# Attention and two MLPs on one Trainium2 core: the shared sums of a seven-product gate and value stage, kept in PSUM by copies on ACT instead of added on DVE

## The chip, the cores and the metric

The kernel runs on one core of one Trainium2 chip. The metric is the device time of one execution in microseconds (us); lower is better. All times below are in us unless marked ns. The engines are TensorE (PE; its weight loads are shown as PEld), VectorE (DVE), ScalarE (ACT), GpSimd (POOL) and SyncE (SP), whose queue issues the DMAs.

## The reference

With N = 6016 tokens and C = 256 channels, attention over the channels is followed by a squared-ReLU MLP (256 to 2048 to 256) and by a gated MLP (256 to 1536 to 256) with an RMS norm ahead of it:

```python
qn = q / (np.linalg.norm(q, axis=1, keepdims=True) + 1e-06)
kn = k / (np.linalg.norm(k, axis=1, keepdims=True) + 1e-06)
a = softmax(kn.transpose(0, 2, 1) @ qn / tau)      # 256 x 256
x = (v @ a).reshape(6016, 256)
h = np.maximum(x @ w_in, 0.0)
x = h * h @ w_out
xn = x / np.sqrt(np.mean(x * x, axis=-1, keepdims=True) + 1e-06) * rms_g
g = xn @ w_gate
out = (g / (1 + np.exp(-g)) * (xn @ w_val)) @ w_out2
```

Every product is carried at nearly full float32 precision by three TensorE matmuls: each operand is split in a high and a low part, and high times high, high times low and low times high are summed in PSUM.

## The kernel before

The tokens are cut into 12 blocks: ten of 512 tokens and two of 448 (lines 46 to 52). The attention runs first, then the first MLP block by block (`mlp1`), then the second MLP (`mlp2`) over six pairs of blocks. The order of all work is written out by hand (line 54); every engine runs its instructions in the order in which the code issues them.

**The second MLP.** A pair p holds two blocks of equal size n, the two columns of a 2 x 2 block product: gate and value (the rows) of two token blocks, over two halves of the channels. Seven products stand for the eight of the plain form: A11, S2, S3, S1, A12, A22 and S4 (line 882). Their operands on the token side are prepared by `pair_steps` (lines 841 to 877), written to DRAM as a high and a low part, and read back by `fetch` (lines 895 to 906). `group(f)` (line 926) runs the seven products of one of the 12 slices of 128 hidden features. A product is three matmuls into one PSUM bank (`product`, line 930; line 933).

The four results are the two gate columns and the two value columns. Two of them need a sum that is shared: u = A11 + S2, and u + S3. In the kernel before, ACT copies A11 out of its bank (p1, line 955), DVE adds S2 (u, line 961), adds u and S3 and S1 to form the second value (h22, lines 963 and 967), adds u and S3 + A22 to form the first value (h21, line 973), multiplies it by the first SiLU (line 974), and adds u and S1 + S4 to form the second gate (h12, line 978). A12 accumulates onto A11, A22 onto S3 and S4 onto S1, by matmuls that do not start anew (lines 969, 972, 976).

**What comes after a group.** A group's second half is done by steps that stand in the next group (`late`, line 948): ph1 and pl1 split h21 in a high part (ACT, line 984) and a low part (DVE, line 988), silu2 applies SiLU to h12 (ACT, line 994), p2 multiplies it onto h22 (DVE, line 997) and splits its high part (ACT), pl2 its low part (DVE). Only then can the down projection use them: a "down" is three matmuls (lines 103 to 105) for one of two token blocks and one of two output halves, so a group makes four. They are put on a list and taken off it in the four `down_slot` calls of each group (line 886); one that is made in group f is taken in the later slots of group f+1 or in the first slots of group f+2. When the last group of a pair is taken down, ACT copies each of the four results out of PSUM (line 922), which falls in the first two groups of the next pair.

**The start of the second MLP (pair 0).** Three downs of the first MLP are still pending; the first three slots of group 0 take them, six matmuls of 448 columns each (line 764). The fourth slot of group 0 and the first two of group 1 are empty. The token operands of the seven products have the numbers 0 (for A11), 1 (S2), 2 (S3), 3 (S1), 4 (A12), 5 (A22) and 6 (S4), the first argument of `product`. They are loaded through SP's queue, each by two DMAs (high and low part): 0, 1 and 2 are issued in the last block of the first MLP (line 1136), 3 to 6 behind them at its end (line 1146). SP works in order. The load of index 2 writes tiles o4 and o5, which the norm of the block before last holds until its last scaling on DVE (line 833). After each of the first eight groups of pair 0, two more steps are done (lines 1150 to 1169): the norm of the last block (`norm_steps`, lines 776 to 839: copies and squares on ACT after group 0, sum, transposition and reduction on DVE after group 1, the mean by a small matmul, the square root on ACT and its spreading after group 2, the scaling on DVE after group 3), then the preparation of the last pair's operands after groups 4 to 7 (`pair_steps`). Each of those seven preparations is a cast on ACT (line 856), a subtraction on DVE (line 863) and a write to DRAM (line 866); the tile has two buffers, so ACT can cast the third only when the first has been written.

**PSUM.** Eight banks: four rotate under the name mm (line 63), two each hold the two sums of the down projection.

Of the kernel before, what the change touches and what calls it, by code (L numbers as in the profile page):

```python
# [14 lines left out]
ALU = mybir.AluOpType  # L15
# [4 lines left out]
NB = 512  # L20
# [5 lines left out]
def attn_moe_kernel(ctx: ExitStack, tc, q, k, v, tau, w_in, w_out, w_gate, w_val, w2, rms_g, out):  # L26
# [8 lines left out]
    nc = tc.nc  # L35
# [27 lines left out]
    def mm():  # L63
        return ps.tile([P, NB], F32, tag="mm", name="mm", bufs=4)
# [24 lines left out]

    few = wp.tile([P, P], F32, name="few")  # L90
    eps, g_sb, tau_sb, rden = few[:, 0:1], few[:, 16 : 16 + KC], few[:, 32:33], few[:, 48 : 48 + KC]
    nc.gpsimd.memset(eps, 1e-6)


    wo_h = wp.tile([P, NF1, C], F32R, tag="wo_h", name="wo_h")
# [675 lines left out]

    SLOT = ((0, 4), (2, 6))
    xst, x_dram = {}, {}
    norm_small = ctx.enter_context(tc.tile_pool(name="ns", bufs=1, reuse_waits="tile"))

    def norm_steps(b, y):
# [3 lines left out]
        st = {}  # L780
# [32 lines left out]
            )  # L813

        def s4():
            ms = mm()[:, :G]
            nc.tensor.matmul(ms, mw, st["sm"][0], start=True, stop=True)

            def root():
                x, r = st["sm"]  # L820
                nc.scalar.activation(out=x, in_=ms, func=AF.Sqrt, bias=eps)
                nc.vector.reciprocal(out=r, in_=x)

            return root
# [55 lines left out]


    A11, A12, A22, S1, S2, S3, S4 = range(NC7)
    slots = {"n": 0}
    waiting = []

    def down_slot():
# [18 lines left out]
        for j in range(2):  # L905
            nc.sync.dma_start(out=f32(ops[i][j]), in_=x_dram[p][:, i, j, :n])

    def mlp2(p, ops, after_product, after_group):
        n = blocks[2 * p][1]
        o = {}  # L910
        left = []
# [14 lines left out]
        def group(f):  # L926
            c = gv[f // 2]
            fs = slice(f % 2 * P, (f % 2 + 1) * P)

            def product(i, a, bank, start):  # L930
                xh, xl = ops[i]
                for j, (hl, x) in enumerate(((0, xh), (1, xh), (0, xl))):
                    nc.tensor.matmul(bank, c[:, hl, a, fs], x, start=start and j == 0, stop=j == 2,  # L933
                                     skip_group_check=not start)
                after_product(f, i)


            b0, b1 = mm()[:, :n], mm()[:, :n]
            if f % 2:
                b0, b1 = b1, b0  # L940
            b2, b3 = mm()[:, :n], mm()[:, :n]
            pu = wp.tile([P, 2, NB], F32, tag="raw", name="pu", bufs=NRAW)[:, :, :n]
            p1, u = pu[:, 0], pu[:, 1]
            hp = wp.tile([P, 2, NB], F32, tag="gp", name="hp", bufs=2)[:, :, :n]
            h21, h22 = hp[:, 0], hp[:, 1]
            old = left.pop() if left else {}

            def late(k):
                if k in old:
                    old[k]()  # L950

            add, dve = nc.vector.tensor_tensor, nc.vector.tensor_tensor
            product(0, A11, b0, True)
            late("ph1")
            nc.scalar.copy(out=p1, in_=b0)
            late("silu2")
            late("pl1")
            down_slot()
            product(1, S2, b1, True)
            late("p2")  # L960
            add(out=u, in0=b1, in1=p1, op=ALU.add)
            product(2, S3, b2, True)
            add(out=h22, in0=b2, in1=u, op=ALU.add)  # L963
            late("pl2")
            down_slot()
            product(3, S1, b3, True)
            add(out=h22, in0=b3, in1=h22, op=ALU.add)
            down_slot()
            product(4, A12, b0, False)
            sg1 = wp.tile([P, NB], F32, tag="dg", name="sg", bufs=3)[:, :n]  # L970
            nc.scalar.activation(out=sg1, in_=b0, func=AF.Silu)  # L971
            product(5, A22, b2, False)
            add(out=h21, in0=b2, in1=u, op=ALU.add)  # L973
            dve(out=h21, in0=sg1, in1=h21, op=ALU.mult)  # L974
            down_slot()
            product(6, S4, b3, False)
            h12 = wp.tile([P, NB], F32, tag="dg", name="sg", bufs=3)[:, :n]
            add(out=h12, in0=b3, in1=u, op=ALU.add)
            new = {}
            parts = {}  # L980

            def hi(t, x):
                parts[t] = work("sh", n), work("sl", n)
                nc.scalar.copy(out=parts[t][0], in_=x)  # L984

            def lo(t, x):
                ph, pl = parts[t]
                dve(out=pl, in0=x, in1=f32(ph), op=ALU.subtract)  # L988
                due = slots["n"] + 2
                waiting.extend((due, down(f, t, d, ph, pl)) for d in range(KC))  # L990

            new["ph1"] = lambda: hi(0, h21)
            new["pl1"] = lambda: lo(0, h21)
            new["silu2"] = lambda: nc.scalar.activation(out=h12, in_=h12, func=AF.Silu)

            def p2():
                dve(out=h22, in0=h12, in1=h22, op=ALU.mult)
                hi(1, h22)

            new["p2"] = p2  # L1000
            new["pl2"] = lambda: lo(1, h22)
            left.append(new)
            after_group(f)
# [150 lines left out]
    for p in range(NP):  # L1154
# [16 lines left out]
                for i in range(3):  # L1171
                    fetch(p + 1, i, nxt)

        group, left, rest, finish = mlp2(p, ops, after_product, after_group)
        if tails:
            left.append(tails[0])
        for f in range(NF2):
# [42 lines left out]
```

## Time and profile before

| what | value |
|---|---|
| median of 3 runs | 1152.65 us (1152.17 to 1152.69) |
| the profiled execution | 1152.68 us |
| its span in the profile | 1150.9 us |
| TensorE, DVE, ACT busy | 98%, 75%, 58% of the span |
| granted TensorE clock, mean | 0.996 |
| first MLP ends, second MLP begins | about 595.6 us |

The profile shows one execution. Its span runs from the first to the last instruction; the execution's own time is 1.8 us longer. In the rows of its views, an instruction or a group of equal neighbours stands with its start, its duration, engine, line, operation and the tiles that it writes and reads; in square brackets stands how long the engine was idle before it and what ended that. Matmuls overlap: a matmul's duration is longer than the distance to the next one. Tiles of the program: mm is a PSUM bank of the products, acc one of the down sums, sh and sl the high and low part of a hidden tile, hp holds h21 and h22, pu holds p1 and u, sg a SiLU or h12, o and xs are loaded operands, gv the weights of gate and value, xp a prepared operand and xd its copy in DRAM.

### The profile page before, as it was taken

How to read it: one execution, taken by the hardware profiler on the slowest of the kernel's cores; microseconds unless marked ns; L12 is line 12 of the kernel's file. 1: busy time of each engine (PE TensorE's matmuls, PEld its weight loads, DVE VectorE, ACT ScalarE, POOL GpSimd, SP SyncE). 2: the span in 40 equal slices, each digit the busy share in tenths (PEclk: the TensorE clock that was granted, in tenths of full speed). 3: DMA queues.
4: the chain of work that ended last, by engine and by line, in shares of the span. 5: the costliest groups of instructions: out<-in, count | busy, mean ns of one | idle time of the engine just before them, and what ended most of it. 6: DMA issues, size and time to landing. Idle time of an engine off the chain costs nothing.

```text
span 1150.9 us, 14618 instructions
## 1 busy us (share of the span) xinstructions
PE 1123.1 (98%) x5220; PEld 942.2 (82%) x5220; DVE 868.9 (75%) x1372; ACT 666.4 (58%) x1166; POOL 57.5 (5%) x91
## 2 busy tenths in 40 slices
PE   8999989999999999999999899999999999999996
PEld 7978868878888888889977678888888888888995
DVE  6987868877787665565658787887877887877875
ACT  7687878678687676676665344334334334334432
POOL 1021130201201000000000000000000000000000
PEclk9999999999999999999999999999999999999999
DMA  9852332442351320120146222302302302202101
GB/s 290 229 144 87 89 87 74 131 152 83 110 174 46 109 75 17 56 90 1 76 160 277 81 87 73 92 1 74 92 1 74 92 1 74 72 14 64 25 13 32
DMA packets 99289, 101.23 MB, mean 88 GB/s; under 512 B 57616, under 2 KB 74256, under 8 KB 98704
## 3 DMA queue, kind: packets, MB, share of 16 engines
q1 hardware_dynamic: 99216, 100.29, 27.5%
q8 instruction: 41, 0.67, 0.2%
q14 instruction: 32, 0.26, 0.1%
HBM read 65.21 MB, written 35.06 MB: 87 GB/s over the span
## 4 chain that ended last, share of the span: by engine, by line
PE 82%; DVE 7%; ACT 5%; DMA 3%; SPq 2%; issue 2%; POOL 1%; DVEq 0%; ACTq 0%; POOLq 0%
PE mm L933 27%; PE acc L104 11%; PE acc L103 11%; PE acc L105 11%; PE mm L104 6%; PE mm L103 6%; PE mm L105 6%; DMA xd<-xp 1%; SPq L379 1%; ACT o L739 1%; DMA qraw<-in_k_dram 1%; DVE dg L141 1%; DVE sl L751 1%; ACT o L743 1%; PE mm L541 1%
## 5 line engine op out<-in xcount | busy, mean ns | idle before, releaser
L933 PE MATMUL mm<-o,gv 128*128 128x512 f32 (+1 forms) x1188 | 309.8, 388 | 4.7 <-DVE hp L963 3.2
L933 PEld LDWEIGHTS mm<-o,gv 128*128 128x128 f32 x1188 | 222.1, 188 | 51.7 <-DVE hp L963 5.5
L751 DVE TENSOR_TENSOR sl<-o,sh 128x512 fp32r<-128x512 f32 (+1 forms) x192 | 133.5, 695 | 112.7 <-ACT sh L744 99.5
L984 ACT CAST sh<-hp 128x512 fp32r<-128x512 f32 (+1 forms) x144 | 88.2, 612 | 151.4 <-DVE hp L974 97.4
L104 PE MATMUL acc<-sl,wo_h 128*128 128x512 f32 (+1 forms) x384 | 149.0, 388 | 3.6 <-DVE sl L751 3.6
L103 PE MATMUL acc<-sh,wo_h 128*128 128x512 f32 (+1 forms) x384 | 149.6, 389 | 1.6 <-ACT sh L747 1.5
L105 PE MATMUL mm<-o,m_l 128*128 128x512 f32 (+1 forms) x384 | 148.1, 386 | 0.3 <-DVE m_l L678 0.3
L105 PE MATMUL acc<-sh,wo_l 128*128 128x512 f32 (+1 forms) x384 | 148.2, 386 | 0.2
L103 PE MATMUL mm<-o,m_h 128*128 128x512 f32 (+1 forms) x384 | 148.0, 385 | 0.0
L104 PE MATMUL mm<-o,m_h 128*128 128x512 f32 (+1 forms) x384 | 148.0, 385 | 0.0
L739 ACT ACTIVATE o<-mm 128x512 f32<-128x512 f32 (+1 forms) x192 | 112.4, 585 | 60.0 <-PE mm L105 55.6
L971 ACT ACTIVATE sg<-mm 128x512 f32<-128x512 f32 (+1 forms) x72 | 42.5, 590 | 140.9 <-PE mm L933 140.8
L103 PE MATMUL acc<-sh,w_h 128*128 128x512 f32 (+1 forms) x288 | 111.3, 386 | 2.4 <-ACT sh L984 2.4
L104 PE MATMUL acc<-sl,w_h 128*128 128x512 f32 (+1 forms) x288 | 111.4, 387 | 0.7 <-DVE sl L988 0.6
L105 PE MATMUL acc<-sh,w_l 128*128 128x512 f32 (+1 forms) x288 | 110.9, 385 | 0.0
L988 DVE TENSOR_TENSOR sl<-hp,sh 128x512 fp32r<-128x512 f32 (+1 forms) x144 | 96.4, 669 | 10.4 <-ACT sh L984 6.3
L973 DVE TENSOR_TENSOR hp<-mm,pu 128x512 f32<-128x512 f32 (+1 forms) x72 | 48.9, 679 | 64.4 <-PE mm L933 64.4
L104 PEld LDWEIGHTS acc<-sl,wo_h 128*128 128x128 f32 x384 | 72.1, 188 | 19.3 <-DVE sl L751 6.7
L103 PEld LDWEIGHTS acc<-sh,wo_h 128*128 128x128 f32 x384 | 72.1, 188 | 16.4 <-ACT sh L747 2.8
L105 PEld LDWEIGHTS mm<-o,m_l 128*128 128x128 f32 x384 | 72.1, 188 | 14.6 <-DVE m_l L678 1.1
L105 PEld LDWEIGHTS acc<-sh,wo_l 128*128 128x128 f32 x384 | 72.1, 188 | 14.2 <-DVE wo_l L170 0.9
L103 PEld LDWEIGHTS mm<-o,m_h 128*128 128x128 f32 x384 | 72.1, 188 | 13.6
(139 smaller groups left out, 1770.6 us busy)
## 6 DMA issues: line engine op xcount, KB each, us to landing
xd<-xp SPq DMA_DIRECT2D x35, 512.0 KB, 2.6
o<-xd SPq DMA_DIRECT2D x58, 256.0 KB, 4.4
raw<-in_moe_w_out_dram SPq DMA_DIRECT2D x14, 512.0 KB, 3.7
gv<-gvd SPq DMA_DIRECT2D x4, 1792.0 KB, 14.7
gvd<-gp SPq DMA_DIRECT2D x12, 512.0 KB, 3.4
out_dram<-ot SPq DMA_DIRECT2D x40, 128.0 KB, 2.5
qraw<-in_q_dram SPq DMA_DIRECT2D x13, 384.0 KB, 4.8
qraw<-in_k_dram SPq DMA_DIRECT2D x13, 384.0 KB, 5.9
```

The costliest lines, as they stand in the source:

```text
L103: nc.tensor.matmul(o, wh, xh, start=start, stop=False)
L104: nc.tensor.matmul(o, wh, xl, start=False, stop=False)
L105: nc.tensor.matmul(o, wl, xh, start=False, stop=stop)
L141: nc.vector.tensor_tensor(out=gi, in0=gi, in1=self.raw[:, 0::2], op=ALU.add)
L379: nc.sync.dma_start(out=rows[:, g, kk], in_=src[:, kk])
L739: nc.scalar.activation(out=r, in_=o, func=AF.Relu)
L751: nc.vector.tensor_tensor(out=sl, in0=s, in1=f32(sh), op=ALU.subtract)
L933: nc.tensor.matmul(bank, c[:, hl, a, fs], x, start=start and j == 0, stop=j == 2, skip_group_check=not start)
L971: nc.scalar.activation(out=sg1, in_=b0, func=AF.Silu)
L973: add(out=h21, in0=b2, in1=u, op=ALU.add)
L984: nc.scalar.copy(out=parts[t][0], in_=x)
L988: dve(out=pl, in0=x, in1=f32(ph), op=ALU.subtract)
```

## The change

The products of a group are issued in another order, and the shared sums stay in PSUM.

- New order: A11, S1, slot, S2, A12, slot, S3, slot, slot, A22, S4. Before: A11, slot, S2, S3, slot, S1, slot, A12, A22, slot, S4.
- The four banks: b0 holds A11, then A11 + A12. The other three take turns (over `slots["g"] % 3`) as bh (S1, then S1 + S4), bu (u) and bv (u + S3, then u + S3 + A22).
- ACT copies b0 into bu, and S2's matmuls accumulate onto it without starting anew; ACT then copies bu into bv, onto which S3 and later A22 accumulate, and copies u out to SBUF. After S3 it copies bv out (w). DVE then adds S1 and w (h22), multiplies bv with the first SiLU (h21) and adds S1 + S4 and u (h12): three operations in place of six.
- In the first group of pair 0 alone, one matmul each opens bu and bv before anything accumulates there.
- The mean of the last block's norm, a matmul of 14 columns after group 2, no longer takes a bank of its own out of the rotation: ACT writes zeros to 16 columns of b0 of group 2 after that group's first SiLU, and the small matmul accumulates there. The zeros come from one more memset on POOL at the start.

```diff
--- before.py
+++ after.py
@@ -89,7 +89,9 @@
 
     few = wp.tile([P, P], F32, name="few")
     eps, g_sb, tau_sb, rden = few[:, 0:1], few[:, 16 : 16 + KC], few[:, 32:33], few[:, 48 : 48 + KC]
+    zeros = few[:, 64 : 64 + NB // 32]
     nc.gpsimd.memset(eps, 1e-6)
+    nc.gpsimd.memset(zeros, 0.0)
 
 
     wo_h = wp.tile([P, NF1, C], F32R, tag="wo_h", name="wo_h")
@@ -771,6 +773,8 @@
 
     SLOT = ((0, 4), (2, 6))
     xst, x_dram = {}, {}
+
+    spare = {2: None}
     norm_small = ctx.enter_context(tc.tile_pool(name="ns", bufs=1, reuse_waits="tile"))
 
     def norm_steps(b, y):
@@ -813,8 +817,12 @@
             )
 
         def s4():
-            ms = mm()[:, :G]
-            nc.tensor.matmul(ms, mw, st["sm"][0], start=True, stop=True)
+            if b < NBLK - 1:
+                ms = mm()[:, :G]
+                nc.tensor.matmul(ms, mw, st["sm"][0], start=True, stop=True)
+            else:
+                ms = next(iter(spare.values()))[:, :G]
+                nc.tensor.matmul(ms, mw, st["sm"][0], start=False, stop=True, skip_group_check=True)
 
             def root():
                 x, r = st["sm"]
@@ -880,7 +888,7 @@
 
 
     A11, A12, A22, S1, S2, S3, S4 = range(NC7)
-    slots = {"n": 0}
+    slots = {"n": 0, "g": 0}
     waiting = []
 
     def down_slot():
@@ -905,7 +913,7 @@
         for j in range(2):
             nc.sync.dma_start(out=f32(ops[i][j]), in_=x_dram[p][:, i, j, :n])
 
-    def mlp2(p, ops, after_product, after_group):
+    def mlp2(p, ops, after_product, after_group, spare):
         n = blocks[2 * p][1]
         o = {}
         left = []
@@ -935,12 +943,14 @@
                 after_product(f, i)
 
 
-            b0, b1 = mm()[:, :n], mm()[:, :n]
-            if f % 2:
-                b0, b1 = b1, b0
-            b2, b3 = mm()[:, :n], mm()[:, :n]
+
+
+            turn3 = slots["g"] % 3
+            slots["g"] += 1
+            b0, *b = [mm()[:, :n] for _ in range(4)]
+            bh, bu, bv = b[turn3:] + b[:turn3]
             pu = wp.tile([P, 2, NB], F32, tag="raw", name="pu", bufs=NRAW)[:, :, :n]
-            p1, u = pu[:, 0], pu[:, 1]
+            u, w = pu[:, 0], pu[:, 1]
             hp = wp.tile([P, 2, NB], F32, tag="gp", name="hp", bufs=2)[:, :, :n]
             h21, h22 = hp[:, 0], hp[:, 1]
             old = left.pop() if left else {}
@@ -949,33 +959,43 @@
                 if k in old:
                     old[k]()
 
-            add, dve = nc.vector.tensor_tensor, nc.vector.tensor_tensor
+            add, dve, cp = nc.vector.tensor_tensor, nc.vector.tensor_tensor, nc.scalar.copy
             product(0, A11, b0, True)
+            if p > 0 or f > 0:
+                cp(out=bu, in_=b0)
             late("ph1")
-            nc.scalar.copy(out=p1, in_=b0)
             late("silu2")
             late("pl1")
+            product(3, S1, bh, True)
             down_slot()
-            product(1, S2, b1, True)
+            if p == 0 and f == 0:
+
+                for x in (bu, bv):
+                    nc.tensor.matmul(x, c[:, 0, A11, fs], ops[0][0], start=True, stop=True)
+                cp(out=bu, in_=b0)
+            product(1, S2, bu, False)
+            cp(out=bv, in_=bu)
+            cp(out=u, in_=bu)
             late("p2")
-            add(out=u, in0=b1, in1=p1, op=ALU.add)
-            product(2, S3, b2, True)
-            add(out=h22, in0=b2, in1=u, op=ALU.add)
-            late("pl2")
-            down_slot()
-            product(3, S1, b3, True)
-            add(out=h22, in0=b3, in1=h22, op=ALU.add)
-            down_slot()
             product(4, A12, b0, False)
             sg1 = wp.tile([P, NB], F32, tag="dg", name="sg", bufs=3)[:, :n]
             nc.scalar.activation(out=sg1, in_=b0, func=AF.Silu)
-            product(5, A22, b2, False)
-            add(out=h21, in0=b2, in1=u, op=ALU.add)
-            dve(out=h21, in0=sg1, in1=h21, op=ALU.mult)
+            if f in spare:
+
+                spare[f] = b0[:, : NB // 32]
+                cp(out=spare[f], in_=zeros)
+            late("pl2")
             down_slot()
-            product(6, S4, b3, False)
+            product(2, S3, bv, False)
+            cp(out=w, in_=bv)
+            add(out=h22, in0=bh, in1=w, op=ALU.add)
+            down_slot()
+            down_slot()
+            product(5, A22, bv, False)
+            dve(out=h21, in0=bv, in1=sg1, op=ALU.mult)
+            product(6, S4, bh, False)
             h12 = wp.tile([P, NB], F32, tag="dg", name="sg", bufs=3)[:, :n]
-            add(out=h12, in0=b3, in1=u, op=ALU.add)
+            add(out=h12, in0=bh, in1=u, op=ALU.add)
             new = {}
             parts = {}
 
@@ -1171,7 +1191,7 @@
                 for i in range(3):
                     fetch(p + 1, i, nxt)
 
-        group, left, rest, finish = mlp2(p, ops, after_product, after_group)
+        group, left, rest, finish = mlp2(p, ops, after_product, after_group, spare if p == 0 else ())
         if tails:
             left.append(tails[0])
         for f in range(NF2):
```

## Rows read from the trace of the kernel before

**Rows 1.** The page: TensorE's busy time, and its granted clock in 40 slices.
```profile
PE 1123.1 (98%) x5220; PEld 942.2 (82%) x5220; DVE 868.9 (75%) x1372; ACT 666.4 (58%) x1166; POOL 57.5 (5%) x91
...
PEclk9999999999999999999999999999999999999999
```

**Rows 2.** Busy time by stretch: stretch, length, engines' busy us (instructions), clock, DMA.
```profile
595.60:607.20 11.60, 10.05 (x41) 6.85 (x40) 4.74 (x8) 4.82 (x9) 0.00 (x0) 1.00 0.82 287
607.20:667.20 60.00, 54.01 (x229) 41.78 (x228) 48.48 (x80) 26.47 (x47) 0.00 (x0) 1.00 0.36 150
667.20:1138.00 470.80, 470.80 (x2119) 397.58 (x2118) 378.21 (x601) 191.83 (x342) 0.00 (x0) 1.00 0.18 52
```

**Rows 3.** Timeline of a steady group: start, duration, engine, line, operation, count.
```profile
906.91 0.62 ACT L984 CAST sh<-hp 128x512 fp32r<-128x512 f32 x1 [1.54 <-DVE hp L974]
...
907.43 0.58 ACT L955 COPY pu<-mm 128x512 f32<-128x512 f32 x1
...
911.30 1.52 PE L933 MATMUL mm<-o,gv 128*128 128x512 f32 x6
912.24 0.60 ACT L971 ACTIVATE sg<-mm 128x512 f32<-128x512 f32 x1 [2.32 <-PE mm L933]
...
912.66 0.39 PE L103 MATMUL acc<-sh,w_h 128*128 128x512 f32 x1
```

**Rows 4.** Timeline, first group of pair 0.
```profile
595.60 0.86 PE L933 MATMUL mm<-o,gv 128*128 128x512 f32 x3
...
596.29 0.36 PE L103 MATMUL acc<-sh,wo_h 128*128 128x448 f32 x1
...
596.66 4.88 SPq L906 DMA_DIRECT2D o<-xd  x10
...
597.50 0.86 PE L933 MATMUL mm<-o,gv 128*128 128x512 f32 x3
...
599.52 1.05 PE L933 MATMUL mm<-o,gv 128*128 128x512 f32 x3 [1.15 <-DMA o<-xd]
```

**Rows 5.** Timeline, fourth group of pair 0: a product that waits for DVE.
```profile
627.32 0.69 DVE L963 TENSOR_TENSOR hp<-mm,pu 128x512 f32<-128x512 f32 x1
...
628.07 0.98 PE L933 MATMUL mm<-o,gv 128*128 128x512 f32 x3 [0.98 <-DVE hp L963]
...
628.88 0.40 PE L103 MATMUL acc<-sh,w_h 128*128 128x512 f32 x1
```

**Rows 6.** Groups of instructions by line, 667.2 to 1138.0: busy us, mean ns.
```profile
L967 DVE TENSOR_TENSOR hp<-mm,hp 128x512 f32<-128x512 f32 (+1 forms) x64 | 43.0, 671 | 0.0
...
L955 ACT COPY pu<-mm 128x512 f32<-128x512 f32 (+1 forms) x64 | 36.6, 572 | 0.0
...
L922 ACT COPY ys<-acc 128x512 f32<-128x512 f32 x20 | 11.7, 586 | 12.4 <-PE acc L105 12.4
```

**Rows 7.** Tile xd, 597.9 to 598.1: the two loads of S1's operand.
```profile
L906 SPq DMA_DIRECT2D o<-xd x2: 382/404/426, 597.6 to 598.0; - x2
...
DMA to landing us min/median/max: 4.0/4.3/4.5
```

**Rows 8.** Timeline, fourth and seventh group of pair 0: a table load, a blocked ACT.
```profile
623.96 1.28 ACT L994 ACT_TABLE_LOAD   x1
...
650.01 0.56 ACT L856 CAST xp<-xst 128x448 fp32r<-128x448 f32 x1 [5.50 <-DMA xd<-xp]
...
651.15 0.50 PE L103 MATMUL acc<-sh,w_h 128*128 128x512 f32 x1 [1.20 <-ACT sh L984]
```

**Rows 9.** The page's DMA issues: KB each, median us to landing.
```profile
xd<-xp SPq DMA_DIRECT2D x35, 512.0 KB, 2.6
```

**Rows 10.** Timeline of TensorE near the start of the span.
```profile
8.28 0.50 PE L541 MATMUL mm<-hl 128*128 128x256 f32 x2 [1.91 <-DVE hl L517]
```

**Rows 11.** Busy time by stretch near the start, columns as in rows 2.
```profile
5.30:8.60 3.30, 1.39 (x10) 1.18 (x11) 1.22 (x1) 2.19 (x3) 1.04 (x5) 1.00 0.92 306
8.70:12.00 3.30, 3.30 (x18) 3.30 (x17) 1.83 (x2) 1.57 (x3) 0.00 (x0) 0.50 1.07 362
```

## The prediction

> **What bounds the kernel now.** I read the page's busy times first: TensorE is busy for 98% of the span, at full granted clock [rows 1], so what counts is where it stands still. The stretches of the second MLP show that [rows 2]. From 667.2 to 1138.0 TensorE is busy for 470.80 of 470.80 us; the reader is to see that no faster DVE can shorten this. DVE is busy 80% of it, ACT 41%. All that can be won lies in the first pair: its group 0 (595.60 to 607.20) and its groups 1 to 7 (to 667.20).
>
> Next the pace. Six matmuls of 512 columns take 912.66 - 911.30 = 1.36, one 0.227, so a product or a down (three of them) takes 0.68 and a group of 33 takes 7.48 [rows 3]. Six of 448 columns take 597.50 - 596.29 = 1.21 [rows 4]. Group 0 holds 7 products and three slots of six 448-column matmuls: 4.76 + 3.63 = 8.4 in 11.6, so 3.2 are lost. Groups 1 to 7 hold 7 x 7.48 less the two slots that are empty in group 1 (1.36), 51.0 in 60.0: 9.0 lost. The change can win 12 us at most, and has 470 us without a gap to lose in.
>
> Last the hand-over times. ACT starts 0.26 after a product's last matmul leaves room for the next (912.24 against 911.30 + 0.68) and takes 0.60; a free ACT starts the next operation 0.52 after a 0.62 one [rows 3]. When TensorE has to wait, the next product ends 0.20 + 0.68 after the release: 628.88 against 627.32 + 0.69 [rows 5]. So a release 0.20 ahead of a product's turn costs nothing.
>
> **Steady groups.** The change takes three of nine DVE operations out of a group (0.67 each) and puts three more copies on ACT (eight operations, not five; 0.57 each) [rows 6]. DVE's share hides nothing on TensorE there, so the gain is 0. The new risk is TensorE's wait for ACT. The turns of a group are A11 at 0, S1 0.68, slot 1.36, S2 2.04, A12 2.72, slot 3.40, S3 4.08, two slots 4.76, A22 6.12, S4 6.80.
> - Copy into bu: starts 0.68 + 0.26 = 0.94, ends 1.52, with 0.20 is 1.72 against S2's 2.04.
> - Behind it ACT does ph1 and silu2, to 2.6. Copy into bv: S2 ends 2.72, so 2.98 to 3.56, with 0.20 is 3.76 against S3's 4.08. Copy u, sh of h22 and silu follow, to about 5.06.
> - Copy w: S3 ends 4.76, so 5.02 to 5.60, with 0.20 is 5.80 against A22's 6.12; h22's addition then ends 6.32, with 0.20 is 6.52 against S4's 6.80.
>
> Each is about 0.3 early: cost 0. No row has a copy from PSUM into PSUM. The nearest are 0.58 (PSUM to SBUF) and 0.62 (SBUF to SBUF) [rows 3]; I take 0.58, as it has the same source, with 0.48 (the step between two such operations) and 0.66 (one 0.04 step more) as ends. The slack covers 0.88. Only the second group after each pair's change carries two more ACT copies of 0.59 [rows 6], one of them ahead of copy w: 0.16 lost, five times, **+0.8**. The loads of the next pair keep the distance between a product's turn in one group and in the next (eleven turns), so they cost 0 where they are; the tail's chain is the same. The memset on POOL is alone at the start: 0.
>
> **Group 0.** Here the new order of products counts. SP's queue is not reordered: it issues the loads of S3's operands from 596.66 [rows 4] and S1's two behind them, at 597.6 and 598.0, which land 4.0 and 4.5 later, at 601.6 and 602.5 [rows 7]. S1 is now the second product, not the fourth. A11 ends at 596.28; what hid the load (a slot, S2, S3 and a slot) stands behind S1 in TensorE's queue. S1 starts at 601.8, its third matmul at 602.7, to 602.93; slot to 604.14; the two new matmuls that open bu and bv cost 0.45, to 604.59. The first of them frees the copy into bu: 604.63 to 605.21, and S2 starts at 605.41, 0.82 late. S2, A12, slot, S3, slot, A22, S4 take 5 x 0.68 + 2 x 1.21: to 611.23, where group 0 ended at about 607.2: **+4.1**. The reader sees in the old rows that S3 waited for its load too, 1.15 at 599.52 [rows 4]; S1's landed behind work.
>
> **Groups 1 to 7.** The old stalls were DVE's lateness, and ACT's wait for a buffer: the preparation of the last pair's operands holds ACT until a write has landed (idle 5.50 before 650.01), and TensorE then loses 1.20 and more [rows 8]. That wait stays: the write leaves after DVE's h12 (0.67) and its own subtraction, and takes 2.6 [rows 9]. Counted from the end of S4: 0.26 + 0.60 + 0.62, issue 0.04, landing 2.65, then the cast, next operation 0.50 later, makes 4.67. Behind it stands the copy into bu, to 5.25, so S2 starts at 5.45 instead of 2.04: **3.4 lost in one stretch**, in group 6 and again in group 7. Before, 3.2 were lost in each, in pieces. Group 5 loses 0.7 behind the earlier casts (before 0.45). Group 3's A11 waits for the square root, whose input now lies in b0's bank (0.67), and its S3 for the copy behind the table load of 1.28 [rows 8] (0.45): 1.1, as DVE's wait there cost 1.25 [rows 5]. Group 1's S2 and S3 wait for ACT behind the two copies and two squares of the last norm (0.36 each). Together 9.5 against 9.0: **+0.5**.
>
> **The clock.** Near the start TensorE stood still for 1.91 after sparse matmuls, and the granted clock then fell to 0.50, that is from 2.4 to 1.2 GHz, and stayed for about 3.4 with TensorE busy throughout [rows 10, 11]. The stops of 1.20 in rows 8 left it full. The new stops are 5.5, 3.4 and 3.4, longer than either. Of 3.4 us at the low level half is lost, 1.7. I take one fall for the first stop and one for the other two together: **+3.4**, with 0 and 6 as ends (after the first, up to 2.7 if it lasts on, and 1.7 twice). The Trainium skill ("TensorE: Matmul & The Clock Gate", the practical rules) says the clock drops after a long idle gap between bursts of matmuls. By that rule all three stops would cost and the sum would be an estimated 1.7 higher; the start of this trace agrees, and no stop this long in mid-kernel is in it.
>
> **Sum.** 4.1 + 0.5 + 0.8 + 3.4 = 8.8 on the profiled execution's 1152.68 (median of the runs 1152.65): 1161.5.
>
> **Rivals.**
> - *ACT in time in groups 1 to 7.* DVE has six operations for nine, so the writes could leave and land before ACT asks for the buffer, and the copies would always be done in time. Then all 9.0 lost there go, and with the clock held 1152.7 + 4.1 + 0.8 - 9.0 = 1148.6. It decides at a landing about 1.2 after S4's end; against it stand the 2.6 of a write and DVE's h12 ahead of it. 7%.
> - *Half of that.* The clock holds and the write lands 1.7 sooner in groups 6 and 7: 1152.7 + 5.4 - 3.4 = 1154.7, within 0.2%. For it: DVE comes to h12 without a queue; against it: that is in the 4.67 already. 9%.
> - *A fall of the clock at all three stops*: 1163.2. For it: 1.91 was enough at the start; against it: the matmuls before that stop were sparse, and here dense work stands on both sides of each. This is what the Trainium skill's rule above would give. 20%.
> - *A wait in every group.* If a copy into PSUM takes over 0.88, or its hand-over is that much later, each tenth beyond costs 0.2 in some 70 groups, 14 us: 1175. For it: no row has such a copy; against it: its neighbours are 0.57 to 0.62. 10%.
>
> **Numbers.** A measurement of this kernel tells about 0.2% (2.3 us) from no change. The forecast has 54%. Without any fall of the clock it is 1158.1; with three falls, the first of them the longest, 1164.1, and with copies of 0.66 another 0.8. The range takes these in and reaches down to the second rival: 1155 to 1166. Slower 84% (forecast, third and fourth rival), same 9%, faster 7%.
>
> **What would show it.** In the timeline of after: S1 of group 0 starting at about 601.8 behind a DMA; S2 waiting for ACT by about 3.4 in groups 6 and 7; the granted clock at 0.5 for a stretch after 599; no idle time of TensorE from about 676 on, and ACT about 62% busy there (eight operations of 0.58 in 7.48). If the group lasts over 7.48 in the steady stretch, the hand-over or the copy was mis-sized; if group 0 ends before 609, the loads' landing was; if the second MLP's start loses under 12 in all, the forecast is wrong.

## The result, and the profile after

The changed kernel is slower: 1165.01 us in the median of four runs (1164.57 to 1166.10) against 1152.67 of the kernel before beside it; the ratio is 1.0109, with a 95% interval of 1.0092 to 1.0127. The profiled execution took 1164.76, 12.1 more than the one of before, and lies in the forecast's range. The forecast of 1161.5 is 3.3 short of it.

Read the page first, as in [rows 1]. The copies have moved as meant: DVE is down from 869 to 747 us, ACT up from 666 to 766. TensorE's clock line, which was at 9 in all 40 slices, now has a slice below 9 in mid-span (the 8 at its end lies behind TensorE's last product).

```profile
PE 1129.3 (97%) x5222; PEld 944.9 (81%) x5222; DVE 747.3 (64%) x1156; ACT 765.6 (66%) x1383; POOL 57.4 (5%) x92
...
PEclk9999999999999999999989999999999999999998
```

Then the stretches, as in [rows 2] (stretch, length, busy us and instructions of PE, PEld, DVE, ACT and POOL, granted clock, DMA share, GB/s): group 0, groups 1 to 7, the rest, and three short pieces in which the clock was low.

```profile
595.35:612.58 17.23, 11.87 (x43) 9.13 (x42) 2.80 (x5) 6.30 (x12) 0.00 (x0) 0.80 0.88 329
612.58:677.41 64.83, 56.81 (x228) 43.98 (x227) 37.06 (x59) 37.01 (x69) 0.00 (x0) 0.95 0.25 102
677.41:1150.00 472.59, 472.59 (x2118) 396.51 (x2117) 269.09 (x409) 278.99 (x534) 0.00 (x0) 1.00 0.18 52
599.99:606.82 6.83, 5.25 (x12) 4.01 (x13) 0.00 (x0) 0.57 (x1) 0.00 (x0) 0.50 1.02 368
658.02:661.43 3.41, 3.41 (x10) 2.63 (x9) 1.99 (x3) 2.77 (x6) 0.00 (x0) 0.50 0.00 0
671.67:675.09 3.42, 3.42 (x9) 2.63 (x8) 1.04 (x2) 2.21 (x6) 0.00 (x0) 0.50 0.00 0
```

The third line answers to the 470.80 us of [rows 2]: TensorE is still never idle there, with DVE at 57% in place of 80% and ACT at 59% in place of 41%. The DVE time saved bought nothing. Most of the loss is in the first two lines and in the clock; the 1.9 us of it that lie in the third line, in the changes of pair and in the last pair, do not show as idle time.

A finer measure helps: the length of a group, from the start of its first product (A11) to the start of the next group's. Twelve groups are a pair. Before, the groups 0 to 7 of pair 0 took 11.53, 6.41, 7.84, 8.90, 7.49, 7.95, 10.75 and 10.73; after, 17.23, 6.70, 7.66, 9.76, 7.49, 8.16, 12.53 and 12.54. From group 8 on both take 7.48, but for the places named below. So 12.1 us split into: group 0, 5.7 later; groups 1 to 5, 1.2; groups 6 and 7, 3.6; the second group after each change of pair, 0.14 four times, 0.6; the last pair, 1.3 (6.82 us a group of 448 columns, where it was 6.69); and 0.25 less because group 0 began earlier.

Group 0 in the timeline of TensorE (start, duration, engine, line, operation, tiles, shape, count, and in brackets the idle time before and what ended it), to be read beside [rows 4]:

```profile
595.35 0.86 PE L941 MATMUL mm<-o,gv 128*128 128x512 f32 x3
601.34 1.62 PE L941 MATMUL mm<-o,gv 128*128 128x512 f32 x3 [5.13 <-DMA o<-xd]
...
605.00 1.06 PE L974 MATMUL mm<-o,gv 128*128 128x512 f32 x2
606.29 1.90 PE L941 MATMUL mm<-o,gv 128*128 128x512 f32 x6 [0.23 <-ACT mm L975]
```

A11 runs, then TensorE stands 5.13 us for the load of S1's operand; the granted clock falls to 0.50 during that stop, at 599.99, and what follows runs at half the clock until 606.82. Groups 6 and 7 show the second kind of stop, on ACT and on TensorE:

```profile
656.58 0.56 ACT L864 CAST xp<-xst 128x448 fp32r<-128x448 f32 x1 [5.70 <-DMA xd<-xp]
657.05 0.58 ACT L965 COPY mm<-mm 128x512 f32<-128x512 f32 x1
...
657.68 2.65 PE L941 MATMUL mm<-o,gv 128*128 128x512 f32 x6 [3.13 <-ACT mm L965]
...
670.20 1.70 PE L941 MATMUL mm<-o,gv 128*128 128x512 f32 x6 [3.12 <-ACT mm L965]
```

The cast of the preparation waits 5.70 for its buffer, which a write to DRAM still reads. Behind it in ACT's order stands the copy into bu, which S2 accumulates onto; so TensorE stands 3.1 in one piece. Before, the same blocked cast [rows 8] cost TensorE as much in a group (10.75 less 7.48), but in pieces, of which 1.20 was the longest.

Last the steady groups, for which the forecast set one slack after another. A11 starts at 752.36, S2 at 754.40, S3 at 756.44, A22 at 758.48:

```profile
752.36 0.84 PE L941 MATMUL mm<-xs,gv 128*128 128x512 f32 x3
753.29 0.57 ACT L965 COPY mm<-mm 128x512 f32<-128x512 f32 x1 [2.87 <-PE mm L941]
...
754.40 0.84 PE L941 MATMUL mm<-xs,gv 128*128 128x512 f32 x3
...
755.28 0.57 ACT L977 COPY mm<-mm 128x512 f32<-128x512 f32 x1 [0.35 <-PE mm L941]
...
756.44 0.84 PE L941 MATMUL mm<-xs,gv 128*128 128x512 f32 x3
...
757.32 0.59 ACT L990 COPY pu<-mm 128x512 f32<-128x512 f32 x1
...
758.48 1.52 PE L941 MATMUL mm<-o,gv 128*128 128x512 f32 x6
```

The copies start 0.93, 2.92 and 4.96 after A11 (forecast 0.94, 2.98, 5.02) and each is done about 0.55 before the product that needs it. TensorE never waits.

### The profile page after: what moved, and what is told of

It is laid out like the page before. It is cut to its first block, busy times and chain, and to the rows that moved or that the text cites. A ratio compares the mean times of both kernels' runs of the same rounds, so it can differ in the third digit from the quotient of the medians.

```text
span 1163.0 us, 14400 instructions
## 1 busy us (share of the span) xinstructions
PE 1129.3 (97%) x5222; PEld 944.9 (81%) x5222; DVE 747.3 (64%) x1156; ACT 765.6 (66%) x1383; POOL 57.4 (5%) x92
## 4 chain that ended last, share of the span: by engine, by line
PE 84%; DVE 4%; ACT 3%; DMA 2%; issue 1%; POOL 1%; SPq 0%; DVEq 0%; ACTq 0%; POOLq 0%
PE mm L941 29%; PE acc L106 12%; PE acc L105 12%; PE acc L107 12%; PE mm L107 6%; PE mm L105 6%; PE mm L106 6%; DMA xd<-xp 1%; PE mm L668 1%; DVE sl L753 1%; ACT o L741 1%; DVE dg L147 0%; DVE dg L143 0%; DVE xp L871 0%; DMA o<-xd 0%
## 5 line engine op out<-in xcount | busy, mean ns | idle before, releaser
L941 PE MATMUL mm<-o,gv 128*128 128x512 f32 (+1 forms) x1188 | 306.6, 391 | 13.4 <-ACT mm L965 7.4
L965 ACT COPY mm<-mm 128x512 f32<-128x512 f32 (+1 forms) x71 | 39.9, 562 | 177.9 <-PE mm L941 177.9
L941 PE MATMUL mm<-xs,gv 128*128 128x512 f32 (+1 forms) x324 | 88.7, 382 | 0.0
```

What stands on the lines that cost most here:

```text
L965: cp(out=bu, in_=b0)
```

## The experiments

The theory was that nothing of the loss comes from the copies' own time, and that all of it comes from two places: the new order of products, which puts S1 ahead of its load, and ACT's blocked cast, which now holds a product. Rivals: the additions on DVE would be as late in that order; the clock; the copies themselves. (The group lengths leave out of this theory what group 3 and the changes of pair cost; experiments 4 and 10 come to them.) All experiments change the kernel after, unless told otherwise, and each was run beside the kernel before on the same chip.

**1. The order alone.** The kernel before with its additions on DVE, its products in the new order A11, S1, S2, A12, S3, A22, S4. Nothing is copied into a bank.

```diff
+            product(3, S1, b3, True)
 ...
-            product(2, S3, b2, True)
-            add(out=h22, in0=b2, in1=u, op=ALU.add)
+            product(4, A12, b0, False)
+            sg1 = wp.tile([P, NB], F32, tag="dg", name="sg", bufs=3)[:, :n]
+            nc.scalar.activation(out=sg1, in_=b0, func=AF.Silu)
 ...
-            product(3, S1, b3, True)
+            product(2, S3, b2, True)
+            add(out=h22, in0=b2, in1=u, op=ALU.add)
```

> Theory A (the order of the products exposes the load of S1's operand at the start of the second MLP, whatever forms the sums): group 0 lasts about 17.2 as after the change, with the clock's fall after 599, groups 1 to 7 stay as before the change (60.0 +- 0.6, no second and third fall), so 1158.4. Rival B (the copies on ACT cost the time, the order little): within 1.5 of the kernel before, 1152 to 1154. The last pair's group of 448 columns: 6.69 if the copies set its pace, 6.82 if the order does (1.3 more).

Measured: 1166.49 (1163.09 to 1167.36), ratio 1.0115 (1.0098 to 1.0131): as slow as the whole change. Groups 0 to 7 take 16.26, 6.96, 8.42, 9.38, 7.54, 8.67, 13.08 and 14.01. That groups 1 to 7 would stay as they were, as I had it, is wrong, and so is rival B. The last pair takes 6.69 a group. ACT and TensorE in groups 6 and 7:

```profile
657.43 0.56 ACT L856 CAST xp<-xst 128x448 fp32r<-128x448 f32 x1 [7.03 <-DMA xd<-xp]
...
659.05 0.96 PE L933 MATMUL mm<-o,gv 128*128 128x512 f32 x3 [3.69 <-ACT pu L955]
```

Here no product accumulates onto a copy, and TensorE still stands 3.7 (3.68 in group 7), for the old copy of A11 (p1) behind the same cast: A12, which accumulates onto A11's bank, must not start before the copy has read it, and is now the fourth product, not the fifth. So the new order is enough for the long stops, without any copy into PSUM. It is not the only way to them: the copies in the old order (experiment 8) make them too.

**2. One preparation step after a group, not two.** The steps that the kernel does in pairs after groups 5 to 7 are spread over the later groups.

```diff
-        beside.setdefault(i // 2, []).append(s)
+        beside.setdefault(i // 2 if i < 10 else i - 5, []).append(s)
```

> Theory A (in groups 6 and 7 the bank copies stand on ACT behind casts that wait for a write, and the stop of 3.4 lets the clock fall): with one preparation step a group instead of two no cast waits, groups 5 to 7 last 7.5 to 7.7 and the second and third fall are gone: 1164.8 - 10.8 = 1154.0. Rival B (eight ACT operations and the casts do not fit into a group): part of the stalls stays, spread over groups 5 to 10, above 1159.

Measured: 1155.57 (1155.04 to 1157.19), ratio 1.0026 (1.0015 to 1.0038). Groups 6 and 7 take 7.48 each, as theory A has it: the write has a whole group to land in, the stops are gone, and so are the falls of the clock there. One new stop shows, in the first group of the next pair, which takes 9.23:

```profile
700.13 1.07 PE L941 MATMUL mm<-o,gv 128*128 128x512 f32 x3 [1.35 <-DMA o<-xd]
```

That is S1's load for pair 1. SP issues the loads of xs behind the last step's write, at 692.35, and S1's load behind them, from 694.17. In the combined kernels below the last two steps stay together after group 9 (in experiment 5 the loads of xs go out at 678.81), and the stop is not there.

**3. S1's load before S3's.** The loads of pair 0 are issued nearly in the order in which the new order of products asks for them: those of S1 and A12 go ahead of S3's.

```diff
-            beside = merge(beside, {13: [lambda: [fetch(0, i, ops0) for i in range(2)]], 15: [lambda: fetch(0, 2, ops0)]})
+            beside = merge(beside, {13: [lambda: [fetch(0, i, ops0) for i in range(2)]]})
 ...
-    for i in range(3, NC7):
+    for i in (3, 4, 2, 5, 6):
```

> Theory A (S1's load lands late because it is issued behind S3's on SP's queue, which waits for the norm): issued first, it goes out at about 595.5 and lands from 598.2, S1 starts about 2.8 sooner; 1162 if the clock still falls once there, 1160 if the shorter stop of 2.4 leaves it full. Rival C (the landing is set by the traffic, not by the issue): S1 still starts after 601, 1164.8.

Measured: 1160.46 (1158.60 to 1162.36), ratio 1.0063 (1.0046 to 1.0080). Group 0 takes 13.70 in place of 17.23:

```profile
595.41 0.86 PE L941 MATMUL mm<-o,gv 128*128 128x512 f32 x3
598.46 1.58 PE L941 MATMUL mm<-o,gv 128*128 128x512 f32 x3 [2.19 <-DMA o<-xd]
```

S1 starts 2.9 sooner, and 2.19 of idle time stay, since the load still goes out only at the end of the first MLP. In this execution the clock stayed low for 6.83 us in groups 6 and 7 (13.61 each), so the group, and not the run, is what to read. In group 0 it fell too, for 3.41 us.

**4. The bank zeroed by DVE.** The change lets the norm's mean accumulate onto zeros that ACT writes. Here DVE writes them.

```diff
-                cp(out=spare[f], in_=zeros)
+                nc.vector.memset(spare[f], 0.0)
```

> Theory A (the square root has two waits since ACT itself writes the zeros, the first of them stands ahead of the table load, so its 1.28 is no longer hidden): with the zeros written by DVE the table load starts before the mean's matmul, S2 of group 3 no longer waits 0.9, group 3 lasts 8.8 to 8.9 instead of 9.76. Rival D (the chain of root, reciprocal and copy sets it): group 3 stays at 9.7.

Measured: 1164.41 in one run. Only group 3 matters: 8.60 in place of 9.76, a little below theory A's 8.8 to 8.9. ACT in the timeline of the changed kernel:

```profile
624.60 0.58 ACT L990 COPY pu<-mm 128x512 f32<-128x512 f32 x1
627.16 1.28 ACT L829 ACT_TABLE_LOAD   x1 [1.98 <-PE mm L825]
628.46 0.27 ACT L829 ACTIVATE ns<-mm,few 128x14 f32<-128x14 f32 x1
...
629.51 0.58 ACT L965 COPY mm<-mm 128x512 f32<-128x512 f32 x1
```

And with DVE's zeros:

```profile
625.33 0.58 ACT L990 COPY pu<-mm 128x512 f32<-128x512 f32 x1
625.92 1.28 ACT L829 ACT_TABLE_LOAD   x1
628.09 0.27 ACT L829 ACTIVATE ns<-mm,few 128x14 f32<-128x14 f32 x1 [0.88 <-PE mm L825]
...
629.30 0.58 ACT L965 COPY mm<-mm 128x512 f32<-128x512 f32 x1
```

In the changed kernel ACT stands idle 1.98 and only then loads the table for the square root; with DVE's zeros the load runs inside that idle time. In the kernel before, too, the load ran ahead of the mean's matmul and cost nothing (in its timeline):

```profile
619.86 1.28 ACT L821 ACT_TABLE_LOAD   x1
...
621.56 0.27 ACT L821 ACTIVATE ns<-mm,few 128x14 f32<-128x14 f32 x1 [0.41 <-PE mm L817]
```

Why it moved shows in the trace's semaphore instructions, which the views leave out. The square root of the changed kernel depends on two things, TensorE's mean and ACT's own zeros. The wait for TensorE is an instruction of its own, at 627.12, ahead of the load, and the square root itself carries the wait for ACT. With DVE's zeros there are still two waits, but the one ahead of the load, at 625.61, is for DVE and is met at once (the zeros end at 625.58), and the square root carries the wait for TensorE. Before, there was one wait, carried by the square root. So theory A has the cost right, and its reason only in part: not the number of waits decides, but which of them stands ahead of the load.

**5. All three mends together**, with the copies (experiments 3 and 4, and 2 in this form):

```diff
-        beside.setdefault(i // 2, []).append(s)
+        beside.setdefault(i // 2 if i < 10 else min(i - 5, 9), []).append(s)
```

> The changed kernel with its three start costs taken out (S1's load first, preparation steps one a group up to group 8 and the last two after group 9, zeros by DVE). Theory A: the causes add up: 1155.6 of the run with spread steps, less the 1.75 that its next pair waited for S1's load behind the late loads of xs, less 2.8 to 3.5 for the earlier load, less 1.1 in group 3: 1149.5 +- 1; one fall of the clock at most. Rival B (copies on ACT cost time of themselves): above 1152.7.

Measured: 1147.79 (1147.41 to 1148.56), ratio 0.9957 (0.9942 to 0.9971): faster than the kernel before, and 0.7 below the 1149.5 +- 1 of theory A, which allowed for one fall of the clock. The clock stays full from the first MLP's end to TensorE's last matmul.

**6. The same spreading in the kernel before**, with nothing of the change in it.

> The kernel before with the same spread of the preparation steps and nothing else. Theory A (its stalls in groups 5 to 7 are ACT held by casts): groups 5 to 7 last 7.5 instead of 7.95, 10.75 and 10.73: 1152.7 - 7.0 = 1145.7. Rival E (DVE, with nine operations and the extra ones, stays late in those groups and is the cause): less than half of that, above 1149.

Measured: 1146.72 (1145.85 to 1147.49), ratio 0.9946 (0.9931 to 0.9961). It beats the kernel before, the changed kernel, and, by 1.1 in the median, the changed kernel with all its mends. The ranges of these last two just meet, so the traces decide: from the first to the last the products of the second MLP take 534.9 here and 536.3 in experiment 5. Of the 1.4 between them group 0 makes 0.8 and the changes of pair 0.5. So what made experiment 5 fast is not the change.

**7. The new order, mended, with DVE's additions**: experiment 1 with the mends of 3 and 5 (it has no zeros to write).

> The sums by DVE as before, in the new order of products, with S1's load first and the spread steps. Theory A (what the change costs is its order; copies or additions make no difference to a steady group): within 1.5 of the run all_three, about 1149 to 1150. Rival F (the copies take a wait for DVE off TensorE that the additions have in this order): slower than all_three by over 2.

Measured: 1150.03 (1148.40 to 1150.38), ratio 0.9972 (0.9959 to 0.9984), 2.2 slower than experiment 5 in the median. In its profiled execution the granted clock fell in group 0, for 3.41 us, and in experiment 5 it did not; the run of 1148.40, with the highest mean clock of the six, is 0.6 slower. So the run is no clean measure, and the groups have to be read. The three mended kernels can be laid side by side, by the stretches of groups 1 to 7 and of the rest (columns as above). Experiment 5, the new order with copies:

```profile
607.94:661.44 53.50, 52.67 (x229) 42.01 (x227) 35.72 (x58) 35.74 (x66) 0.00 (x0) 1.00 0.34 141
661.44:1132.00 470.56, 470.56 (x2115) 395.89 (x2114) 269.30 (x410) 278.87 (x534) 0.00 (x0) 1.00 0.18 54
```

Experiment 6, the old order with DVE's additions:

```profile
608.08:661.58 53.50, 52.38 (x229) 42.15 (x227) 47.32 (x78) 26.02 (x46) 0.00 (x0) 1.00 0.37 152
661.58:1132.00 470.42, 470.42 (x2117) 397.11 (x2116) 378.73 (x602) 192.13 (x343) 0.00 (x0) 1.00 0.18 54
```

Experiment 7, the new order with DVE's additions:

```profile
608.01:664.05 56.04, 53.31 (x228) 41.68 (x227) 48.33 (x78) 25.27 (x45) 0.00 (x0) 1.00 0.33 136
664.05:1132.00 467.95, 467.95 (x2104) 394.71 (x2103) 388.36 (x599) 185.21 (x342) 0.00 (x0) 1.00 0.18 54
```

The rest is without idle time in all three. Groups 1 to 7, at a full clock each time, take 53.50 in the old order, 56.04 in the new one, and 53.50 again in the new one with copies. There the copies do what a DVE with three operations fewer a group should do, and win 2.5 us, as rival F has it; but they win them back from the new order, and the change as a whole has nothing left over. One thing is not told apart: experiment 5 also keeps the norm's mean out of the banks' rotation, which this run does not, and 0.9 of the 2.5 lie in group 3, where that could act.

**8. The copies in the old order.** The copies of the change, the products as before: A11, S2, S3, S1, A12, A22, S4.

> Copies on ACT in the order of products of before. Theory A (a copy needs 0.26 + 0.58 + 0.20 = 1.04 between two products that share a sum, and the old order leaves 0.68 and 0): 0.36 ahead of S2 and 1.04 ahead of S3 are lost in every group, a steady group lasts 8.9, about +100 in all: 1245 to 1255. Rival G (TensorE's queue hides such a wait): within 10 of the changed kernel.

Measured: 1253.88 in one run, as theory A has it. A steady group takes 8.75. TensorE's stop in group 6, and then one of the steady groups:

```profile
660.47 1.65 PE L941 MATMUL mm<-o,gv 128*128 128x512 f32 x3 [3.80 <-ACT mm L965]
...
907.22 0.96 PE L941 MATMUL mm<-o,gv 128*128 128x512 f32 x3
908.84 0.96 PE L941 MATMUL mm<-o,gv 128*128 128x512 f32 x3 [0.66 <-ACT mm L975]
```

S2 (907.22) and S3 (908.84) follow each other directly, with the copy of one bank into the other between them. So the copies need the new order, and what experiment 1 found the order to cost is a price of the copies after all. In groups 6 and 7 TensorE stands 3.80 for the copy into bu behind the blocked cast, in the old order.

**9. The changed kernel again**, unaltered, to tell the program from the execution.

> The changed kernel, unaltered, profiled once more, to tell what belongs to the program from what belongs to one execution. If the slower pace of the last pair (6.82 us a group in the changed kernel against 6.69 before) comes with the program, it is 6.82 again; if it is a matter of the execution, 6.69 can come, and the span is then 1.2 us shorter. The three stops belong to the program: group 0 17.2, group 3 9.8, groups 6 and 7 12.5 each (up to 1 us more in a group where the granted clock stays down longer).

Measured: 1160.41, with the kernel before at 1152.97 beside it. Group 0 takes 16.65, group 3 9.73, groups 6 and 7 10.91 each (12.5 was expected), the last pair 6.69. The stretches (columns as above) of its one fall of the clock, and of the 3.4 us behind the stops of groups 6 and 7:

```profile
602.17:605.58 3.41, 3.17 (x8) 2.74 (x9) 0.00 (x0) 0.00 (x0) 0.00 (x0) 0.50 0.99 354
658.02:661.43 3.41, 3.41 (x15) 2.84 (x16) 1.99 (x3) 3.41 (x7) 0.00 (x0) 1.00 0.00 0
668.90:672.30 3.40, 3.40 (x15) 2.81 (x16) 1.99 (x3) 3.40 (x7) 0.00 (x0) 1.00 0.00 0
```

TensorE's stop in group 6, in the timeline:

```profile
657.98 1.65 PE L941 MATMUL mm<-o,gv 128*128 128x512 f32 x6 [3.13 <-ACT mm L965]
```

The stop of group 6 is the same as in the first execution, 3.13 us, but the clock is at 1.00 behind it. The second execution has one fall of 3.41 us where the first had three, and not the slower pace of the last pair: both are matters of the execution (or of the chip that it ran on), not of the program.

**10. One more copy in every group**, in front of copy w, into the tile that copy w then overwrites.

```diff
             cp(out=u, in_=bu)
+            cp(out=w, in_=bu)
```

> The changed kernel with a third copy of the accumulated bank of S1, S2 and A11 on ScalarE in each group (w, which is overwritten later with the value that counts), so that every later ScalarE operation of the group is about 0.48 us later. In the steady groups of the changed kernel the copy of S3's bank ends 0.4 us ahead of A22's first matmul, which must wait for it. Theory A (the slack is what the timeline of the steady groups shows): A22 is late by about 0.1 us and S4 by about 0.05, a steady group takes 7.6 to 7.65 us in place of 7.48, and the run is 8 to 12 us slower than the changed kernel. Rival B (ScalarE catches up within the group, since it is idle 2.9 us of 7.48): 7.48 still, and no change. Rival C (the wait for the late copy costs the fixed 0.2 to 0.36 us of a hand-over): 7.7 to 7.85, 15 to 25 us slower.

Measured: 1170.76 in one run, 10.4 above experiment 9, which ran beside it. A steady group takes 7.55 to 7.57; the second group after a change of pair 8.08 to 8.10, where it took 7.60. In a steady group:

```profile
758.84 0.61 ACT L991 COPY pu<-mm 128x512 f32<-128x512 f32 x1
759.48 0.69 DVE L992 TENSOR_TENSOR hp<-mm,pu 128x512 f32<-128x512 f32 x1 [0.28 <-ACT pu L991]
759.50 0.53 PEld L941 LDWEIGHTS mm<-o,gv 128*128 128x128 f32 x3 [0.17 <-ACT pu L991]
```

TensorE's weight load for A22 now waits for copy w, and that for S4 for h22's addition behind it (0.20 idle). Copy w ends 0.43 later in its group than in the changed kernel (5.98 after A11's start against 5.55), which costs 0.08, so the slack was some 0.35, close to the forecast's 0.3; where the slack is used up, as after a change of pair, the 0.48 of the extra copy costs 0.48. Theory A names the right term, with a smaller size a steady group (4 us in 50 of them) and a larger one at the changes of pair (2 us). That its total came out is partly luck: the clock fell for 6.83 us in group 0, where experiment 9 had 3.41, and once more in group 7 (12.51), which makes 2.9 of the 10.4.

## Why the prediction was right, and where it was off

Term by term, in the profiled execution and in that of experiment 9 (each group against the same group of before):

| part | forecast | profiled | experiment 9 |
|---|---|---|---|
| group 0 | 4.1, and 1.7 of the clock | 5.7 | 5.1 |
| groups 1 to 5 | 0.1 | 1.2 | 1.1 |
| groups 6 and 7 | 0.4, and 1.7 of the clock | 3.6 | 0.3 |
| changes of pair | 0.8 | 0.6 | 0.5 |
| last pair | 0 | 1.3 | 0.0 |
| start of group 0 | 0 | -0.25 | 0.7 |
| sum | 8.8 | 12.1 | 7.8 |

- **Steady groups: right.** Cost 0, ACT 59% busy (62% forecast). The price that no row of before showed, a copy from PSUM into PSUM, was taken as 0.58 and is 0.57 (L965 in the rows above). The rival of a wait in every group falls; experiment 10 shows how near it was.
- **Group 0: right.** S1's start was forecast at 601.8, 6.2 after A11's, as a wait for the load; it came at 601.34, 5.99 after A11's. Without the fall of the clock the group would be some 3.7 longer than before: the changed kernel of experiment 5, with the same stop of 2.2 as experiment 3, took 12.27 without a fall where experiment 3 took 13.70 with one of 3.4 us, so such a fall costs 1.4, and 16.65 less 1.4 is 15.2 against 11.53 (forecast 4.1 longer).
- **Groups 6 and 7: right in mechanism and size.** 3.4 in one stretch was forecast; 3.13 idle and a slowed first product were found, in 10.91 a group where the clock held, 0.2 more than before. Experiments 1 and 8 widen the reason: the new order without a copy into PSUM makes the stop (3.69), and so does the copy into bu in the old order (3.80). Two slips in the working change little: the parts named for groups 1 to 7 add up to 9.3, not 9.5, and the 4.67 takes h12 at 0.60, where its price was given as 0.67.
- **Group 3: this term failed.** The prediction let A11 wait for the square root in b0's bank, and S3 for the copy behind the table load, 1.1 in all in place of 1.25. A11 did not wait (in the timeline it runs from 626.93, the square root from 628.46). What was late is S2, by 0.76, whose copy stands behind the square root's table load:

```profile
630.14 1.66 PE L941 MATMUL mm<-o,gv 128*128 128x512 f32 x6 [0.76 <-ACT mm L965]
```

S3 was late as forecast (0.64 idle for 0.45), behind the SiLU's load. The group got 0.86 longer, not 0.15 shorter; experiment 4 gives it back. The load of [rows 8] is that of the SiLU; the square root's, hidden before at 619.86, had no term in the prediction, and the change moved it behind the mean.
- **The clock: mis-sized, and not one number.** 3.4 was forecast as two falls. The profiled execution had three, at each stop, as in the third rival: 1.6 in each of groups 6 and 7 (12.53 against 10.91), and some 2.0 in group 0, where it lasted 6.83 us (17.23 against 15.2): 5.2. Experiment 9 had one, of 1.4. The rule of the Trainium skill ("TensorE: Matmul & The Clock Gate", Why this matters for your kernels) that the prediction cited, a drop after a long idle gap, agrees with the first execution; in the second, two stops of 3.1 us left the granted clock at 1.00. The start of the trace, which the prediction took as agreeing with it, says little of such a rule: the stop there is 1.91, and the work around it is sparse [rows 10, 11]. With 0 to 6 as ends the prediction bounded it well; a chance for "falls at all three" would better have been a chance for each stop.
- **The last pair: not foreseen.** 1.3 us, with no idle time in it, and not there in experiment 9.
- **The range: in part luck.** The two executions are 12.1 and 7.8 above before, the forecast of 8.8 lies between them, and what parts them is the clock and the last pair. The first result's median lies 1.0 below the top of the range, one of its runs (1166.10) above it, and nearer to the third rival's 1163.2 than to the forecast.
- **DVE's relief: the first rival was wrong as argued.** The write lands hardly sooner for it: the cast of group 6 starts 4.23 after that group's A11, against 4.29 before and the forecast's 4.17. Only in the new order does it help: with DVE's additions there (experiment 1) it is 4.94.

## What to carry to other kernels

Moving an operation to an idler engine can bring nothing where the bound engine is never idle; look for the stretches where it is idle, and price there the order of work that the move needs. When the order of consumers changes, change the order of their loads with it, and look at what stands in front of every new producer in its engine's queue. Here that was a cast that waits for a buffer; the gain lay in spreading the steps around it, and either kernel could have it.

## What was not expected of the hardware

- The same program had the granted clock fall at three stops in one execution and at one in another, though the stops of groups 6 and 7 were as long (3.13 and 3.12 us in both). A stop of 2.2 us lowered it in experiments 3 and 7 and left it full in experiment 5. It stayed at 0.50 for 3.41 or 6.83 us in pair 0, and once, in experiment 8, for 10.24.
- With two waits, the table load stood behind the first of them and ahead of the second, which its instruction carries (experiment 4): 1.28 us, hidden or not. The Trainium skill ("ScalarE: Activation LUTs", What ACT_TABLE_LOAD costs) gives 1.283 us, which agrees, and about 1.38 us more for a drain, which these rows do not show: with DVE's zeros the load starts 0.01 after the copy before it has ended, and in the changed kernel the square root starts 0.02 after the load has.
- ACT copies 512 columns from PSUM into PSUM in 570 to 572 ns and into SBUF in 592 to 593 (the groups of lines below, over the steady stretch of the changed kernel: line, engine, operation, tiles, shapes, count, busy us, mean ns, idle time before).

```profile
L978 ACT COPY pu<-mm 128x512 f32<-128x512 f32 x52 | 30.9, 593 | 0.0
L990 ACT COPY pu<-mm 128x512 f32<-128x512 f32 x52 | 30.8, 592 | 0.0
L977 ACT COPY mm<-mm 128x512 f32<-128x512 f32 x52 | 29.7, 572 | 16.7 <-PE mm L941 16.7
L965 ACT COPY mm<-mm 128x512 f32<-128x512 f32 x52 | 29.6, 570 | 142.2 <-PE mm L941 142.2
```

- Matmuls of 448 columns ran a group of 33 in 6.82 us through the last pair of one execution and in 6.69 in another, at a full granted clock and with the same program. Neither the copies nor the order set it: experiment 2, with copies, has 6.82, experiments 3, 4 and 5, with copies too, and 1, without them, have 6.69. Why stays open.
